# Two local-attention items of a fused attention and two-layer kernel go from the first chunk to the second, and items start every eight steps

## The chip, the cores and the metric

The kernel runs on one core of a Trainium2 chip. The time is device microseconds (us) of one execution, and the number that counts is the median over runs. In the tables and rows PE is the matrix engine (PEld its weight loads), DVE the vector engine, ACT the scalar engine, POOL the GpSimd engine, SP the queue that issues every DMA.

## The reference, cut to what matters

```
q_d, k_d, v_d = means of q, k, v over 4 neighbouring positions     # 576 -> 144 positions
out_d     = softmax(q_d k_d^T / 8) v_d                              # "down" attention
out_local = softmax(where(|i - j| < 4, q k^T / 8, -1e9)) v          # "local" attention
x = repeat(out_d, 4) + out_local            # 4 batches x 8 heads x 576 x 64 -> 2304 x 512
h = x @ w_in;  x = (h - tanh(h)) @ w_out                            # 512 -> 2048 -> 512
out = (sigmoid(x @ w_gate) * (x @ w_val)) @ w_out2                  # 512 -> 1536 -> 512
```

All of it is float32. A product is made as three passes (high x high, high x low, low x high parts).

## The kernel before, in words

The 2304 rows of x are cut into six chunks of 384. For each chunk the first layer runs 16 blocks f: `do_h` makes 12 matmuls of 384 columns (lines 293 to 295, `ab<-x,w`) into one of four PSUM banks called `ab`; ACT takes the tanh (line 718, `t<-ab`), DVE subtracts it (line 306, `t<-ab,t`, which frees the bank), ACT and DVE split the result into high and low part (line 303 `g<-t`, line 306 `g<-t,g`), and two blocks later (`LAG`) `do_y` makes 12 more matmuls (`acc<-g,w`). In this text these are the product matmuls. The second layer follows after the sixth chunk and is not touched.

The attention that makes x runs between the product matmuls. Two heads are a pair, and a batch has four pairs. Its work is a list of 40 **items**: a "d" item (function `down`) does the down attention of one pair, an "l" item (function `local`) does six blocks of 64 rows of local attention, of one pair or of two. An item has a front part, the **scores** on PE (line 403 for d, line 501 for l), and a back part, the **values** on PE (line 464 for d, line 583 for l), with a softmax on DVE and ACT between them. The values need the softmax turned. In the first chunk (`dense`) PE turns it: for an l item `turn` makes two threes of transposes (line 574). In later chunks a DMA does it: DVE sorts the 16-bit halves into a buffer (line 381 `flip<-pl`), SP issues a DMA_TRANSPOSE (line 390), and `join` copies the result back on ACT and DVE (lines 303 and 381, `pt<-flip`, `pdt<-flip`).

Time in the program is counted in **steps** (`tick`): a step follows every six product matmuls, four per block f. `defer(n, ...)` and `chain(n, ...)` put work n steps later; what `chain` brings to a step is written ahead of what `defer` brings. For an l item of a later chunk: scores at step 0, mask and maximum at 2, the exponentials on ACT at 3 (line 561), normalising at 6, the DMA at 8, the join at 12, the values at the first item start from step 14 on. For a d item the join is at 11. PE's order is chosen by a scheduler when the program is built; from the second chunk on, those of ACT, DVE, POOL and SP follow the recorded order.

`work` starts an item when it is due and when the last one is some steps old: `item` returns that distance, seven steps in later chunks, 4 and 6 in the first. `goal` spreads the items over the chunks: before, 8 items run ahead of the first chunk, 10 in it, then 7, 7 and 8 in the second to fourth. When the last item of a chunk's rows is stored, the chunk's x is loaded (`x_load`, line 694); ahead of block 14 the program takes empty steps until that can be done.

`fetch` loads queries and keys of a pair (line 319, `qk`, three buffers) and its values for the down attention (line 324, `vr`). The sums over four neighbours of q and k (`mean_qk`) are one DVE instruction in the first chunk (line 340) and three POOL instructions later (lines 342 to 344); `mean_v` is three more on POOL. There is one buffer `m` for the sums, and `fetch` waits while it is taken. In batch 1, l items cover blocks 0 to 2 of two pairs together, then blocks 3 to 8 of each pair.

Of the kernel before, what the change touches and what calls it, by code (L numbers as in the profile page):

```python
# [29 lines left out]
NQB = S // QB  # L30
# [6 lines left out]
LAST = NC - 1  # L37
# [28 lines left out]
def tile_kernel(ctx: ExitStack, tc: tile.TileContext, qk, vp, v, w1, w2, mask, ident, out):  # L66
# [31 lines left out]
    startup, dense, spare = [True], [True], [0]  # L98
# [16 lines left out]
    now = [0]  # L115
# [3 lines left out]
    def defer(n, fn, *args):  # L119
        events.setdefault(now[0] + n, []).append((fn, args))  # L120
# [10 lines left out]
    def run_later(kind=None, age=0):  # L131
        for x in list(waiting):
            if now[0] >= x[0] + age and kind in (None, x[1]):
                waiting.remove(x)
                x[2]()
# [162 lines left out]
    qks, means, vds, outd = {}, {}, {}, {}  # L298
# [17 lines left out]
    def load_qk(u):  # L316
        if u != (0, NP - 1):
            qks[u] = ap.tile([128, 2, S], F32, tag="qk", bufs=3, name="qk")
        nc.sync.dma_start(out=qks[u], in_=qk[u[0], u[1]])

    def load_v(u):
        vds[u] = ap.tile([72, 2, 128], F32, tag="vd", bufs=2, name="vd")
        vr = ap.tile([72, 2, FAC, 128], F32, tag="vr", name="vr")
        nc.sync.dma_start(out=vr, in_=vp[u[0], u[1]])
        return vr

    def load_pair(u, d):
        load_qk(u)
        vr = load_v(u)
        defer(d, mean_qk, u)  # L330
        defer(d, mean_v, u, vr)

    summed = {}

    def mean_qk(u):
        summed[u] = now[0]
        m = means[u] = ap.tile([128, 2, SD], F32, tag="m", bufs=1, name="m")
        t = qks[u].rearrange("p i (j r) -> p i j r", r=FAC)
        if dense[0]:
            nc.vector.tensor_reduce(out=m, in_=t, op=ALU.add, axis=AX.X)  # L340
        else:
            nc.gpsimd.tensor_tensor(out=m, in0=t[:, :, :, 0], in1=t[:, :, :, 1], op=ALU.add)
            nc.gpsimd.tensor_tensor(out=m, in0=m, in1=t[:, :, :, 2], op=ALU.add)
            nc.gpsimd.tensor_tensor(out=m, in0=m, in1=t[:, :, :, 3], op=ALU.add)
# [141 lines left out]
    def local(us, n):  # L486
        b, p = us[0]
        two = len(us) == 2
        nb_ = LB // len(us)
# [3 lines left out]
        for x in (0, 3, 1, 4, 2, 5):  # L493
# [3 lines left out]
            for h in range(2):  # L497
                r0 = 64 * h
                o0 = 64 - r0 if x >= 3 and four else r0
                bank, at = (sb[x // 3], x % 3) if four else (sb[0], x)  # L500
# [1 line left out]
                    out=bank[o0:o0 + 64, at, :], lhsT=t[r0:r0 + 64, 0, QB * j:QB * j + QB],  # L502
                    rhs=t[r0:r0 + 64, 1, w0:w0 + WIN], start=True, stop=True,
                )
        if n + nb_ == NQB:
            for u in us:
                done_with(u)
        elif not two:
            pass
# [123 lines left out]
    items = []  # L633
    for b in range(B):
        for p in range(0, NP, 2):
            us = ((b, p), (b, p + 1))
# [5 lines left out]
    items[:n_first + 2] = [x for x in items[:n_first + 2] if x[0] == "d" or x[2] == 0] + [  # L642
        x for x in items[:n_first + 2] if x[0] == "l" and x[2]
    ]
    started, fetched, last_fetch = [0], [n_first + 2], [-9]
    live = {(0, p) for p in range(NP - 1)}

    def done_with(u):
        live.discard(u)
# [5 lines left out]
    def fetch():  # L655

        while not startup[0] and fetched[0] < min(len(items), started[0] + 6):
            x = items[fetched[0]]
            if x[0] == "d" and x[1] != (0, 0):
                if len(live) == 3 or len(vds) == 2 or len(means) == 1 or now[0] < last_fetch[0] + 6:  # L660
                    break
                last_fetch[0] = now[0]
                live.add(x[1])
                load_pair(x[1], 4)
            fetched[0] += 1

    def item():

        fetch()
        x = items[started[0]]  # L670
        if x[0] == "d" and (x[1] not in means or now[0] < summed[x[1]] + (0 if startup[0] else 5 if dense[0] else 2)):
            return 0
        started[0] += 1
        run_later()
        if x[0] == "d":
            down(x[1])
            if not dense[0]:
                fetch()
            return 4 if dense[0] else 7
        local(*x[1:])  # L680
        return 6 if dense[0] else 7

    def needed(c):

# [135 lines left out]
    while any(((1, 0), k) not in xt for k in range(KD)):  # L820
        keep_warm(2)
        if started[0] < n_first:
            x = items[started[0]]
# [185 lines left out]
    for c in range(NC):  # L1009
        if c == 0:  # L1010
            in_order(E.SP)
        elif c == 1:
            in_order(E.SP, E.Activation, E.DVE, E.Pool)
            flip_room()
        first = started[0]
        dense[0] = c == 0
        goal = max(needed(min(c + 1, LAST)), first + (len(items) - first) // max(LAST - 1 - c, 1))
        if c == LAST:
            goal = len(items)
        beat[0] = lambda a=(now[0], first, goal, c): work(*a)  # L1020
        for f in range(NE if c == 0 else 0, F1):
            if f == 14 and c < LAST:
                while x_left[c + 1]:
                    tick()
                x_load(c + 1, xd[c + 1])
            do_h(c, f)
            if c == 0 and f == NE:
                todo += [(0, e) for e in range(NE)]
            todo.append((c, f))
            while len(todo) > LAG:  # L1030
                do_y(*todo.pop(0))
# [219 lines left out]
    for j in range(NJ):  # L1251
        for p in range(len(PAIRS)):
            cycle[:] = now[0], p
            for side in range(2):
# [10 lines left out]
                for n, (a, b, at) in enumerate(PRODUCTS):  # L1265
                    for k in range(2):
                        x = xform[p, k, b]
# [47 lines left out]
    for q, (p, e) in enumerate(passes):  # L1315
        ends = None
        for i in range(NJ if q < len(passes) - 1 else NJ - 1):
# [6 lines left out]
            for n, (a, b) in enumerate(order_b):  # L1324
                for m in both:
                    x, w = u_forms[p, m, b], w_sets[e, m]
# [86 lines left out]
```

## Time and profile before

| | |
|---|---|
| median of 3 runs | 911.87 us (911.01 to 913.51) |
| profiled execution | 912.07 us, its span 910.3 us |
| PE busy | 898.2 us (99%) |
| DVE, ACT, POOL busy | 620.7, 463.8, 169.3 us |
| granted PE clock | 0.999 of full speed |
| DMA | 151.13 MB, 166 GB/s on average |

The span is what the engines show from the first to the last instruction; about 1.8 us of the execution lie around it. PE counts as busy while an instruction of it is in the pipeline, so a busy PE can still start its instructions later than it could: how far apart they start is read from the timeline.

### The profile page before, as it was taken

What the parts mean: (1) busy time and instruction counts of PE and PEld (TensorE: products, weight loads), DVE (VectorE), ACT (ScalarE), POOL (GpSimd) and SP (SyncE); (2) the same over time, 40 slices, a digit from 0 to 9 for tenths busy, and PEclk for the clock granted to TensorE, in tenths of its full rate; (3) what the DMA queues carried; (4) which work ended last, traced back from release to release, by engine and by line L of the source; (5) the groups of instructions that cost most, each with busy time, mean ns of one, the idle gap of its engine ahead of it and who ended that gap; (6) DMA issues with size and microseconds to landing.
All of it is one profiled execution on the core that took longest, in us unless ns stands there. A gap on an engine that the chain in (4) does not pass through costs nothing.

```text
span 910.3 us, 16518 instructions
## 1 busy us (share of the span) xinstructions
PE 898.2 (99%) x6260; PEld 865.4 (95%) x6260; DVE 620.7 (68%) x1063; ACT 463.8 (51%) x1128; POOL 169.3 (19%) x186
## 2 busy tenths in 40 slices
PE   7999999999999999999999999999999999999998
PEld 7788989999899999999999999999999999999998
DVE  5799975655554656567865587676858678978581
ACT  4887865444544545434544545353444446655440
POOL 2321110302222020000032352313131323200000
PEclk9999999999999999999999999999999999999999
DMA  8476656353454544468422235343425268896961
GB/s 294 148 239 232 226 158 127 93 123 91 104 117 112 118 98 99 163 235 311 140 67 68 72 137 173 121 154 122 168 107 179 99 206 304 311 313 232 342 201 37
DMA packets 106927, 151.13 MB, mean 166 GB/s; under 512 B 41104, under 2 KB 92896, under 8 KB 102496
## 3 DMA queue, kind: packets, MB, share of 16 engines
q1 hardware_dynamic: 106848, 150.08, 51.7%
q8 instruction: 49, 0.80, 0.4%
q14 instruction: 30, 0.25, 0.1%
HBM read 97.76 MB, written 43.65 MB: 155 GB/s over the span
## 4 chain that ended last, share of the span: by engine, by line
PE 85%; issue 5%; ACT 3%; DVE 3%; DMA 2%; POOL 1%; SPq 1%; POOLq 0%; DVEq 0%; ACTq 0%
PE ab L293 13%; PE acc L293 13%; PE ab L294 13%; PE ab L295 13%; PE acc L295 13%; PE acc L294 12%; PE ab L583 2%; PE ab L501 1%; ACT pl L561 1%; PE ab L403 1%; PE acc L816 1%; PE ab L464 1%; POOL t L1065 1%; DMA u<-t 1%; DMA o<-o 1%
## 5 line engine op out<-in xcount | busy, mean ns | idle before, releaser
L293 PE MATMUL acc<-g,w 128*128 128x384 f32 x384 | 130.7, 342 | 0.0
L293 PE MATMUL ab<-x,w 128*128 128x384 f32 x376 | 129.6, 345 | 0.6 <-DVE t L306 0.6
L295 PE MATMUL acc<-g,w 128*128 128x384 f32 x384 | 129.7, 338 | 0.0
L294 PE MATMUL acc<-g,w 128*128 128x384 f32 x384 | 129.2, 336 | 0.0
L294 PE MATMUL ab<-x,w 128*128 128x384 f32 x376 | 126.5, 336 | 0.0
L295 PE MATMUL ab<-x,w 128*128 128x384 f32 x376 | 126.4, 336 | 0.0
L306 DVE TENSOR_TENSOR t<-ab,t 128x384 f32<-128x384 f32 x94 | 52.0, 553 | 101.6 <-ACT t L718 100.3
L718 ACT ACTIVATE t<-ab 128x384 f32<-128x384 f32 x94 | 45.7, 486 | 120.3 <-PE ab L295 117.1
L295 PE MATMUL ab<-x,f 128*128 128x384 f32 x261 | 87.8, 336 | 0.9 <-DVE f L1127 0.9
L293 PE MATMUL ab<-x,f 128*128 128x384 f32 x261 | 87.8, 337 | 0.0
L293 PE MATMUL acc<-x,f 128*128 128x384 f32 x261 | 87.7, 336 | 0.0
L295 PE MATMUL acc<-x,f 128*128 128x384 f32 x261 | 87.7, 336 | 0.0
L294 PE MATMUL ab<-x,f 128*128 128x384 f32 x261 | 87.6, 336 | 0.0
L294 PE MATMUL acc<-x,f 128*128 128x384 f32 x261 | 87.6, 336 | 0.0
L306 DVE TENSOR_TENSOR g<-t,g 128x384 fp32r<-128x384 f32 x96 | 57.3, 598 | 31.8 <-ACT g L303 30.8
L303 ACT ACTIVATE g<-t 128x384 fp32r<-128x384 f32 x96 | 50.0, 522 | 48.0 <-DVE t L306 48.0
L293 PEld LDWEIGHTS ab<-x,w 128*128 128x128 f32 x376 | 70.6, 188 | 3.8 <-issue 1.0
L293 PEld LDWEIGHTS acc<-g,w 128*128 128x128 f32 x384 | 72.1, 188 | 1.8 <-issue 1.0
L295 PEld LDWEIGHTS acc<-g,w 128*128 128x128 f32 x384 | 72.2, 188 | 0.4 <-issue 0.2
L294 PEld LDWEIGHTS acc<-g,w 128*128 128x128 f32 x384 | 72.2, 188 | 0.3 <-issue 0.2
L294 PEld LDWEIGHTS ab<-x,w 128*128 128x128 f32 x376 | 70.7, 188 | 0.1
L295 PEld LDWEIGHTS ab<-x,w 128*128 128x128 f32 x376 | 70.7, 188 | 0.0
(193 smaller groups left out, 2019.2 us busy)
## 6 DMA issues: line engine op xcount, KB each, us to landing
raw<-in_w SPq DMA_DIRECT2D x34, 1024.0 KB
u<-t SPq DMA_DIRECT2D x51, 192.0 KB
qk<-in_qk SPq DMA_DIRECT2D x16, 576.0 KB
x<-u SPq DMA_DIRECT2D x9, 960.0 KB
o<-o SPq DMA_DIRECT2D x18, 448.0 KB
u<-c SPq DMA_DIRECT2D x39, 192.0 KB
u<-c SPq DMA_DIRECT2D x18, 384.0 KB
o<-f SPq DMA_DIRECT2D x6, 896.0 KB
```

Source lines behind the costliest of these rows:

```text
L293: nc.tensor.matmul(out=o, lhsT=wh, rhs=xh, start=first, stop=False, **kw)
L294: nc.tensor.matmul(out=o, lhsT=wh, rhs=xl, start=False, stop=False, **kw)
L295: nc.tensor.matmul(out=o, lhsT=wl, rhs=xh, start=False, stop=last, **kw)
L303: nc.scalar.activation(out=dst, in_=src, func=ACTF.Copy)
L306: nc.vector.tensor_tensor(out=dst, in0=a, in1=b, op=ALU.subtract)
L403: nc.tensor.matmul(out=sd[t][o0:o0 + 64, at, :], lhsT=qd[r0:r0 + 64, 40 * j:40 * j + 64], rhs=kd[r0:r0 + 64, :], start=True, stop=True,)
L464: nc.tensor.matmul(out=ob[64 * h:64 * h + 64, :], lhsT=vd[:, f, 64 * h:64 * h + 64], rhs=pdt[:, f, h].rearrange("p j k -> p (j k)"), start ...
L501: nc.tensor.matmul(out=bank[o0:o0 + 64, at, :], lhsT=t[r0:r0 + 64, 0, QB * j:QB * j + QB], rhs=t[r0:r0 + 64, 1, w0:w0 + WIN], start=True, ...
L561: nc.scalar.activation(out=pl[:, j, :], in_=pl[:, j, :], func=ACTF.Exp, bias=nb[:, j:j + 1], accum_out=ssum[:, j:j + 1],)
L583: nc.tensor.matmul(out=ob[r0:r0 + 64, QB * x:QB * x + QB], lhsT=vw[0][:, j - n, i, r0:r0 + 64], rhs=pt[:, x, o0:o0 + 64], start=True, stop ...
L718: nc.scalar.activation(out=t, in_=hb[:, :N], func=ACTF.Tanh)
L816: nc.tensor.matmul(out=idle[:, :128], lhsT=id_sb, rhs=id_sb, start=True, stop=True)
```

## The change

The l items of batch 1, pairs 0 and 1, blocks 3 to 8 (`away`), leave their place and stand directly ahead of the same items of pairs 2 and 3, in the second chunk. The q and k of the two pairs are given up after their first l item (`done_with`) and loaded a second time. From the second chunk on `goal` is the whole list and the distance of items is eight steps. A pair is loaded while the one buffer for sums is still taken, and the sum waits for it (`mean_qk_when_free`).

```diff
@@ load_pair @@
-        defer(d, mean_qk, u)
+        defer(d, mean_qk_when_free, u)
         defer(d, mean_v, u, vr)
...
+    def mean_qk_when_free(u):
+        if len(means) == 1:
+            defer(1, mean_qk_when_free, u)
+        else:
+            mean_qk(u)
@@ local @@
-        if n + nb_ == NQB:
+        if n + nb_ == NQB or us == ((1, 0), (1, 1)):
             for u in us:
                 done_with(u)
@@ the list of items @@
+    away = [("l", ((1, p),), 3) for p in range(2)]
+    rest = [x for x in items if x not in away]
+    at = rest.index(("l", ((1, 2),), 3))
+    items[:] = rest[:at] + away + rest[at:]
@@ fetch @@
             x = items[fetched[0]]
+            if x in away:
+                if len(live) == 3 or now[0] < last_fetch[0] + 6:
+                    break
+                last_fetch[0] = now[0]
+                live.add(x[1][0])
+                load_qk(x[1][0])
             if x[0] == "d" and x[1] != (0, 0):
-                if len(live) == 3 or len(vds) == 2 or len(means) == 1 or now[0] < last_fetch[0] + 6:
+                if len(live) == 3 or len(vds) == 2 or dense[0] and len(means) == 1 or now[0] < last_fetch[0] + 6:
                     break
@@ item @@
-            return 4 if dense[0] else 7
+            return 4 if dense[0] else 8
         local(*x[1:])
-        return 6 if dense[0] else 7
+        return 6 if dense[0] else 8
@@ the chunks @@
-        if c == LAST:
+        if c:
             goal = len(items)
```

Counted over the whole program, PE has 12 transposes fewer (line 574), DVE one sum fewer and four copies more, POOL three additions more, SP two loads of q and k (576 KB each) and two DMA transposes more. Lines of the changed kernel after the first edit have numbers 6 to 16 higher.

First place: DVE at the end of the first chunk, from the scores of its last l item on. Before, the mask of that item's scores (line 538) stands behind the sum of the next pair (line 340):

```order
L306 TENSOR_TENSOR g<-t,g 128x384
L420 TENSOR_REDUCE nb<-ab 128x1
L420 TENSOR_REDUCE nb<-ab 128x2
L340 TENSOR_REDUCE m<-qk 128x288
L538 SCALAR_TENSOR_TENSOR pl<-ab,mask_sb 128x210 x2
L357 RECIPROCAL ss<-ss 128x3
L557 TENSOR_REDUCE nb<-pl 128x6
L359 TENSOR_TENSOR pd<-pd,ss 128x432
```

In the changed kernel (line 538 is 544, 557 is 563, 359 is 365):

```order
L306 TENSOR_TENSOR g<-t,g 128x384
L363 RECIPROCAL ss<-ss 128x3
L365 TENSOR_TENSOR pd<-pd,ss 128x432
L544 SCALAR_TENSOR_TENSOR pl<-ab,mask_sb 128x210 x2
L264 TENSOR_TENSOR w<-raw,w 128x1024
L306 TENSOR_TENSOR t<-ab,t 128x384
L563 TENSOR_REDUCE nb<-pl 128x6
L306 TENSOR_TENSOR g<-t,g 128x384
```

The sum is no longer there; it is made by POOL in the second chunk. Between mask and maximum a step of the weights' preparation (line 264) and a product's subtraction now stand.

Second place: ACT in the fourth chunk, around the join of the last d item (`pdt<-flip`) and the exponentials (line 561, 567 in the changed kernel) of the l item after it. Before:

```order
L718 ACTIVATE t<-ab 128x384
L561 ACTIVATE pl,ss<-pl,nb 128x70 x6
L353 ACTIVATE ss<-ss 128x6
L303 ACTIVATE g<-t 128x384
L303 ACTIVATE pdt<-flip 72x2x2x48 x3
L718 ACTIVATE t<-ab 128x384
```

In the changed kernel:

```order
L303 ACTIVATE od<-ab 128x144
L303 ACTIVATE g<-t 128x384
L303 ACTIVATE pdt<-flip 72x2x2x48 x3
L567 ACTIVATE pl,ss<-pl,nb 128x70 x6
L359 ACTIVATE ss<-ss 128x6
L734 ACTIVATE t<-ab 128x384
```

The join has moved from behind the six exponentials to ahead of them.

Third place: SP from the last store of the second chunk's rows (`x_101<-xo`) on. Before:

```order
L310 DMA x_101<-xo 128x2x192
L694 DMA xs<-x_101 128x384 x4
L310 DMA y_86<-y 128x384 x2
L390 DMA_TRANSPOSE flip<-flip 128x12x128
L310 DMA y_86<-y 128x384 x2
```

In the changed kernel (the load of x is line 710):

```order
L310 DMA x_101<-xo 128x2x192
L710 DMA xs<-x_101 128x384 x4
L319 DMA qk<-in_qk 128x1152
L310 DMA y_86<-y 128x384 x2
L396 DMA_TRANSPOSE flip<-flip 128x12x128
L310 DMA y_86<-y 128x384 x2
```

The second load of pair 1's q and k stands behind the load of x; it goes into the buffer that pair 0's moved item has just read.

## Rows read from the trace of the kernel before

**Rows 1.** The page: the span.
```profile
span 910.3 us, 16518 instructions
```
**Rows 2.** Busy by stretch: PE, PEld, DVE, ACT, POOL (instructions), clock, DMA share, GB/s.
```profile
47.00:130.00 83.00, 82.60 (x750) 73.02 (x749) 75.63 (x123) 66.31 (x204) 13.97 (x15) 1.00 0.66 221
134.00:372.00 238.00, 236.83 (x1962) 223.08 (x1962) 135.60 (x295) 117.92 (x411) 37.61 (x42) 1.00 0.46 107
```
**Rows 3.** PE timeline: start, duration, name, count. Values alone, then (293 us) scores alone.
```profile
204.75 0.34 PE L295 MATMUL ab<-x,w 128*128 128x384 f32 x1
205.02 0.92 PE L583 MATMUL ab<-pt,vw 70*64 70x64 f32 x24
205.87 0.44 PE L293 MATMUL ab<-x,w 128*128 128x384 f32 x1
...
293.34 0.34 PE L295 MATMUL ab<-x,w 128*128 128x384 f32 x1
...
294.13 0.45 PE L293 MATMUL ab<-x,w 128*128 128x384 f32 x1
```
**Rows 4.** PE timeline: values and scores as a pair.
```profile
354.48 0.34 PE L295 MATMUL ab<-x,w 128*128 128x384 f32 x1
354.75 0.92 PE L583 MATMUL ab<-pt,vw 70*64 70x64 f32 x24
...
356.13 0.45 PE L293 MATMUL acc<-g,w 128*128 128x384 f32 x1
```
**Rows 5.** PE timeline: the same two, each in two parts, between two products.
```profile
187.50 0.34 PE L294 MATMUL acc<-g,w 128*128 128x384 f32 x1
...
189.55 0.45 PE L295 MATMUL acc<-g,w 128*128 128x384 f32 x1
```
**Rows 6.** PE timeline: one three of transposes in the first chunk.
```profile
90.87 0.34 PE L294 MATMUL ab<-x,w 128*128 128x384 f32 x1
91.04 0.49 PE L574 MATMUL ab<-id_sb,pl 128*70 128x128 f32 x3
91.29 0.42 PE L293 MATMUL acc<-g,w 128*128 128x384 f32 x1
```
**Rows 7.** PE timeline, end of the first chunk.
```profile
125.34 0.34 PE L293 MATMUL acc<-g,w 128*128 128x384 f32 x1
...
126.20 0.34 PE L295 MATMUL acc<-g,w 128*128 128x384 f32 x1
...
129.43 0.45 PE L293 MATMUL ab<-x,w 128*128 128x384 f32 x1
```
**Rows 8.** DVE timeline just ahead of that place.
```profile
121.25 1.34 DVE L340 TENSOR_REDUCE m<-qk 128x288 f32<-128x1152 f32 x1
```
**Rows 9.** PE timeline, second and third chunk: a product, then an item's values.
```profile
242.50 0.34 PE L295 MATMUL acc<-g,w 128*128 128x384 f32 x1
243.43 0.45 PE L293 MATMUL ab<-x,w 128*128 128x384 f32 x1 [0.60 <-DVE t L306]
...
248.57 0.34 PE L295 MATMUL ab<-x,w 128*128 128x384 f32 x1
249.14 1.27 PE L583 MATMUL ab<-pt,vw 70*64 70x64 f32 x24 [0.23 <-ACT pt L303]
```
**Rows 10.** PE timeline: values of two d items.
```profile
170.09 0.72 PE L464 MATMUL ab<-pdt,vd 72*64 72x144 f32 x8
...
345.51 1.30 PE L464 MATMUL ab<-pdt,vd 72*64 72x144 f32 x8
```
**Rows 11.** DVE timeline ahead of 243.43 us.
```profile
239.24 1.14 DVE L306 TENSOR_TENSOR g<-t,g 128x384 fp32r<-128x384 f32 x1 [2.39 <-ACT g L303]
```
**Rows 12.** Groups of DVE instructions, 130 to 375 us: count | busy, mean ns | idle before.
```profile
L306 DVE TENSOR_TENSOR g<-t,g 128x384 fp32r<-128x384 f32 x50 | 29.9, 598 | 26.1 <-ACT g L303 25.7
```
**Rows 13.** SP and POOL timeline: a load of q and k, and its first reader.
```profile
172.48 0.36 SPq L319 DMA_DIRECT2D qk<-in_qk  x1
177.73 0.70 POOL L342 TENSOR_TENSOR m<-qk 128x288 f32<-128x288 f32 x1 [14.26 <-DMA qk<-in_qk]
```

## The prediction

> **What bounds the kernel now.** I read the busy times by stretch first, because the change touches only the stretch from the first chunk to the end of the attention. In the first chunk PE is busy for 82.60 of 83.00 us, in the three chunks behind it for 236.83 of 238.00 us [rows 2]. So PE is the bound, DVE (75.63 of 83.00 us in the first chunk) comes next there, and the idle time of PE in both stretches is 1.57 us. That is not the whole loss, since a busy PE can start late, so I read PE's timeline next. Product matmuls start 0.172 us apart: five intervals from 125.34 to 126.20 us [rows 7]. Wherever attention stands between two of them, its price is the time from the start of the last product matmul ahead to the start of the first one behind, less 0.17 us. Values alone cost 205.87 - 204.75 - 0.17 = 0.95 us, scores alone 294.13 - 293.34 - 0.17 = 0.62 us [rows 3]. As a pair they cost 356.13 - 354.48 - 0.17 = 1.48 us, 0.09 less than apart [rows 4]; with both torn in two they cost 189.55 - 187.50 - 0.17 = 1.88 us, 0.40 more than the pair [rows 5]. A three of transposes costs 91.29 - 90.87 - 0.17 = 0.25 us [rows 6]. What lies above such a price is a stall.
>
> Behind 372 us the program is the same but for a few steps, so the whole effect has to come out of those 325 us.
>
> **The stalls of before.** I went through all 61 places with attention between products; four stand out.
> - End of the first chunk: 129.43 - 126.20 - 0.17 = 3.06 us for the values of a d item (0.72 as a row [rows 10]), two threes of transposes (0.50) and values (0.95), together 2.17. Stall 0.9 us [rows 7]. Ahead of it DVE makes a sum of 1.34 us while the mask of the last item waits behind it [rows 8].
> - At 242.50 us PE starts its next product 0.93 us later, 0.76 too late, because DVE had not freed the bank; ahead of it a DVE subtraction took 1.14 us [rows 9, 11].
> - At 248.57 us the values come 0.57 us behind the product instead of 0.27 (204.75 to 205.02), and then take 1.27 us instead of 0.92: stall 0.65 us [rows 3, 9].
> - At 345.51 us the values of a d item take 1.30 us, at 170.09 us they took 0.72: stall 0.58 us [rows 10].
>
> Together 2.9 us. This and the prices above are all that can be won.
>
> **The change part by part.**
>
> *PE's own work.* Two l items lose their PE transposes: four threes, -1.0 us. All else that PE computes stays, but stands elsewhere. I gave each place in both orders the price of its rows. From the second chunk on, before, scores or values stood alone at eleven places and were torn at three; with eight steps between items, exactly two blocks, values and scores fall together every time, in the middle of a product's 12 matmuls. The sum there is 33.6 us before. The two items that arrive add 2 x (0.95 + 0.62) = 3.1, which makes 36.7; after, it is 35.0, so pairing gives -1.7 us. In the first chunk the sum is 23.0 before, 18.9 without the two items and their transposes, and 20.8 after, because its scheduler now tears more pieces: +1.9 us. The three together: -0.8 us. The bounds are +0.9 (pairing gives nothing) and -2.7 (the torn pieces of the first chunk cost what whole ones do); I take -0.8, since every place has a price of its own.
>
> *The end of the first chunk.* Two l items fewer for DVE, and the sum of 1.34 us goes to POOL, so the last item's mask no longer waits behind it. The stall of 0.9 is shorter than that sum. In its place a weight subtraction stands between mask and maximum, so I take -0.7 us, between -0.9 and 0.
>
> *Eight steps instead of seven.* A step is six product matmuls, 6 x 0.172 = 1.03 us. Values follow their scores by two items, 16 steps instead of 14, so the chain between them has 2.06 us more. The stalls at 248.57 and 345.51 us, 0.65 and 0.58, are waits for the end of that chain. In addition the join of a d item now stands ahead of the next item's exponentials on ACT and not behind them, as the second place of the order shows. Both should go: -1.23 us. The wait at 242.50 us is DVE being late by 0.76; with one step more per item DVE has 1.03 us more for the same work, but POOL's sums can meet DVE again (below). I take -0.5, between -0.76 and 0.
>
> *What is added and hidden.* Two loads of q and k. The second is the tight one: it starts when the first moved item's scores are done and is read by the next item's scores, 48 product matmuls or 8.3 us later. A load reached its reader 177.73 - 172.48 = 5.25 us after its issue [rows 13]. Hidden, with 3.0 us to spare; without that cover PE would stand for what is missing, at most 5.25 us, and SP, with the stores of y queued behind the load, would pass the delay on to the buffers of y. The two additional DMA transposes and four DVE copies meet a DVE that is busy for 135.60 of 238.00 us in that stretch, the three additional POOL additions a POOL busy for 37.61 [rows 2]: nothing, unless they meet a DVE operation on which PE waits.
>
> *The end of the fourth chunk.* The list now ends later: the load of the fifth chunk's x has to wait four empty steps for its last store. The values of the last item but one stand 28 product matmuls (4.8 us) behind the last item's scores, and ahead of their join on ACT lie that item's six exponentials. I put +0.2 us here, between 0 and 3 (rivals).
>
> Sum: -0.8 - 0.7 - 1.23 - 0.5 + 0.2 = -3.0 us. The profiled execution took 912.07 us, of which 910.3 are its span [rows 1]; it stands 0.2 above the median of 911.87. The forecast by the profile is a span of 907.3, an execution of 909.0, and as a median 911.87 - 3.0 = **908.9 us**.
>
> **DVE and POOL.** At 239.24 us a DVE subtraction took 1.14 us while POOL was adding [rows 11]; the mean of its 50 like is 0.598 us [rows 12]. The Trainium skill, page "SBUF — State Buffer", section "Who interferes with whom", says that a DVE instruction with two inputs from SBUF and a GpSimd instruction that reads SBUF exclude each other for the whole instruction, and that a reduction on trn2 never contends. The long subtraction agrees. The rule speaks against this change, which turns one DVE reduction into three POOL additions and keeps seven other sums on POOL: by it one more stall like the one of now may come, 0.76 + 0.65 us, and the sum would be -1.6; by the rows, where seven sums together leave PE idle for 1.2 us at most, it is nothing. The last rival is this mechanism at its full size, priced from rows.
>
> **The rivals.**
> - *The POOL stalls stay.* The sums meet DVE as they do now, so the waits at 242.50 and 248.57 us keep their 0.76 and 0.65. For it: nothing in the change keeps POOL and DVE apart. Against: one step more per item. The sum becomes -3.0 + 0.5 + 0.65 = -1.85: 910.0 us.
> - *The short end takes it back.* The last item but one has only 70 product matmuls and a pair between its scores and values, 70 x 0.172 + 1.48 = 13.5 us. At 248.57 us an item with 84 matmuls, 84 x 0.172 + 1.48 = 15.9 us, was 0.65 too late, so by that measure this one is 2.4 + 0.65 = 3.0 us late. Against it: in the empty steps no tanh or split of a product stands between the parts of the chain. Then -3.0 - 0.2 + 3.0 = -0.2: 911.7 us.
> - *Slower: every sum on POOL costs PE what one costs now.* All items now lie in the same place of a block. If the sums meet DVE in the place that delays the bank, each costs 0.76 + 0.65 = 1.4 us. With n of the eight the time is 911.87 - 3.0 - 0.26 (what the sum still holds of the wait at 242.50 us) + 1.4 n: slower by over 0.3% from n = 5 on, and 919.8 us with all eight. Against it: 42 POOL instructions, seven sums of six, stand in a stretch in which PE is idle for 1.2 us in all [rows 2], so six of seven cost next to nothing.
>
> **How the numbers follow.** The measurement tells a change of about 0.3%, 2.7 us, from none. The forecast holds 0.50, with a range of its own from 907.5 to 910.0, and so is faster than 909.1 in about three cases of four. The POOL stalls have 0.24, the short end 0.14, the slower rival 0.10; 0.02 are for a late load. Faster: 0.38 from the forecast and 0.05 of the first rival, 0.43. Slower: 0.10, and 0.03 for the short end or the load with more than I gave them, 0.13. The same: 0.44. The range goes from 907.2 (all stalls gone, and pieces of the first chunk cheaper than priced) to 912.4 (the short end and some of POOL); what is outside is the slower rival and the tails.
>
> **What would show it.** PE: no transposes of two of the ten l items of the first chunk; from the second chunk on all attention in pairs of 1.3 to 1.6 us, 48 product matmuls apart, with no row of values longer than 0.92 (l) or 0.72 (d). At the end of the first chunk the time from the d item's values to the next product is as long as its pieces. The moved items' scores start without a wait. It would be wrong if product rows wait for `t` on DVE next to POOL rows, if the values near the end of the fourth chunk carry a wait for `pt`, or if the first chunk's PE work grew by more than priced.

## The result, and the profile after

The changed kernel takes 919.58 us, median of four runs (917.93 to 920.99), against 912.27 us (911.01 to 913.51) for the kernel before beside it: ratio 1.0079, 95% interval 1.0054 to 1.0105. It is slower by 7.3 us where 3 us of gain were forecast. The profiled execution took 918.36 us, 1.2 less than the median; its span is 916.3 us, where [rows 1] has 910.3.

First, busy time by stretch, the two stretches of [rows 2] and one of the second layer, with the same columns, and then this third stretch in the kernel before:

```profile
47.00:130.00 83.00, 82.55 (x654) 71.28 (x653) 72.16 (x112) 61.18 (x175) 11.24 (x13) 1.00 0.64 215
134.00:372.00 238.00, 237.76 (x2045) 226.13 (x2046) 140.93 (x306) 121.99 (x436) 42.92 (x48) 1.00 0.51 119
...
525.00:785.00 260.00, 253.28 (x1449) 252.06 (x1448) 193.45 (x300) 118.86 (x191) 82.57 (x91) 0.99 0.46 163
```

```profile
525.00:785.00 260.00, 260.00 (x1499) 259.13 (x1498) 195.49 (x304) 122.50 (x195) 83.60 (x91) 1.00 0.48 167
```

In the two stretches that the change was meant for PE is as busy as before or busier: 237.76 of 238.00 us, where 236.83 stood. The loss is in the third stretch, from 525 us on, which the prediction did not look at. There PE was busy for all of the 260 us in the kernel before; now it is idle for 6.72 us of them.

Second, the last product of the first layer, on PE's timeline, in the kernel before and then in the changed kernel:

```profile
510.01 0.34 PE L295 MATMUL acc<-g,w 128*128 128x384 f32 x1
```

```profile
507.04 0.34 PE L295 MATMUL acc<-g,w 128*128 128x384 f32 x1
```

It starts 2.97 us earlier. So up to here the forecast of 3.0 us came true in this execution. From here to the end of the span it was 910.3 - 510.01 = 400.3 us; now it is 916.3 - 507.04 = 409.3 us. Those 9.0 us, less the 3.0, are the 6.0 by which the span grew. I call the second number the **rest** and give both for every run.

Third, PE's waits in the changed kernel behind the first layer. There are two, of 3.03 and 3.69 us, and both are new. On PE's timeline the brackets give the wait and what ended it:

```profile
527.83 0.34 PE L295 MATMUL ab<-x,f 128*128 128x384 f32 x1
531.20 0.45 PE L293 MATMUL ab<-x,f 128*128 128x384 f32 x1 [3.03 <-DVE two L1061]
...
541.19 0.34 PE L293 MATMUL ab<-x,f 128*128 128x384 f32 x1
545.23 0.45 PE L294 MATMUL ab<-x,f 128*128 128x384 f32 x1 [3.69 <-DVE x L1009]
...
546.64 0.52 PE L295 MATMUL ab<-x,f 128*128 128x384 f32 x1
546.96 0.52 PE L293 MATMUL ab<-x,f 128*128 128x384 f32 x1
...
549.84 0.34 PE L293 MATMUL ab<-x,f 128*128 128x384 f32 x1
```

These are the first products of the second layer (`x` is the first layer's result in the forms that the second layer multiplies, `f` its weights). The first wait costs 531.20 - 527.83 - 0.17 = 3.20 us, the second 545.23 - 541.19 - 0.17 = 3.87 us. Behind the second, ten products from 546.64 to 549.84 us start 0.32 us apart and not 0.172: another 1.48 us. The window of that stretch shows why, in its granted clock (the 0.66):

```profile
545.00:550.00 5.00, 4.77 (x18) 4.78 (x19) 3.04 (x5) 0.49 (x1) 3.54 (x3) 0.66 0.58 219
```

3.20 + 3.87 + 1.48 = 8.55 of the 9.0 us of this execution.

Fourth, what PE waited for. DVE's timeline in the changed kernel ahead of the first wait's end, and ahead of the second's:

```profile
526.78 1.37 DVE L1009 TENSOR_TENSOR x<-t,x 128x384 fp32r<-128x384 f32 x1
528.07 1.34 DVE L1009 TENSOR_TENSOR x<-xs,x 128x384 fp32r<-128x384 f32 x1
529.34 1.34 DVE L1002 TENSOR_TENSOR x<-t,x 128x384 fp32r<-128x384 f32 x1
530.60 0.54 DVE L1061 TENSOR_TENSOR two<-ab,two 128x384 f32<-128x384 f32 x1
...
540.79 1.56 DVE L1108 TENSOR_TENSOR c<-c 128x768 f32<-128x768 f32 x1
...
542.74 1.09 DVE L1009 TENSOR_TENSOR x<-t,x 128x384 fp32r<-128x384 f32 x1
543.76 0.95 DVE L1108 TENSOR_TENSOR c<-c 128x768 f32<-128x768 f32 x1
544.63 0.55 DVE L1009 TENSOR_TENSOR x<-xs,x 128x384 fp32r<-128x384 f32 x1
```

and in the kernel before (line 993 there is 1009 here, 986 is 1002, 1092 is 1108, 1045 is 1061) ahead of the second place:

```profile
538.95 0.71 DVE L993 TENSOR_TENSOR x<-t,x 128x384 fp32r<-128x384 f32 x1
...
540.05 0.54 DVE L993 TENSOR_TENSOR x<-xs,x 128x384 fp32r<-128x384 f32 x1
540.52 0.95 DVE L1092 TENSOR_TENSOR c<-c 128x768 f32<-128x768 f32 x1
```

`x<-t,x` and `x<-xs,x` make the forms of x; `c<-c` is the second layer's gating product; `two<-ab,two` takes a finished sum out of a PSUM bank and so frees it. DVE takes its work in program order. At the second place that order differs. Before, `x<-t,x` and `x<-xs,x` stand ahead of both gating products. Now the first stands behind one of them and the second behind both, and PE's wait ends with that second one (544.63 + 0.55). From the first form there to the end of this one DVE takes 8.0 us (537.19 to 545.18), where it took 5.2 (535.38 to 540.59).

At the first place the order differs too, but DVE takes no longer. PE's wait ends with `two` (530.60 + 0.54). The first form there and `two`, in the kernel before, and the first form in the changed kernel:

```profile
520.68 1.77 DVE L993 TENSOR_TENSOR x<-xs,x 128x384 fp32r<-128x384 f32 x2 [2.46 <-ACT x L303]
...
530.42 0.54 DVE L1045 TENSOR_TENSOR two<-ab,two 128x384 f32<-128x384 f32 x1
```

```profile
520.94 2.42 DVE L1009 TENSOR_TENSOR x<-xs,x 128x384 fp32r<-128x384 f32 x2
```

From one to the other it is 10.3 us before and 10.2 now. But counted from the last product of the first layer it starts at 13.9 us and not at 10.7, and this 3.2 us is the wait. At both places DVE's rows in the changed kernel leave no gap from the first form to the end of PE's wait, so what starts late there ends late.

The cause of both lies in the program. The forms are made by the preparation of the second layer (`second_weights` and `forms_of_x`, which proceed step by step beside the first layer, at a rate `RATE`). `work` lets it begin when the last attention x has been stored. With the items' distance at eight steps the list ends later: counted in the program, the preparation now begins at step 328 and not 324, while the fifth chunk begins at 322 and not 321. Against PE that is three steps, of 1.03 us each, less of a lead (at the last loads of y, at step 474 and not 471, it is two, since the products stand a step later too). That was the theory to test.

### The profile page after: what moved, and what is told of

It is laid out like the page before. It is cut to its first block, busy times and chain, and to the rows that moved or that the text cites. A ratio compares the mean times of both kernels' runs of the same rounds, so it can differ in the third digit from the quotient of the medians.

```text
span 916.3 us, 16519 instructions
## 1 busy us (share of the span) xinstructions
PE 897.9 (98%) x6248; PEld 864.3 (94%) x6248; DVE 629.7 (69%) x1066; ACT 462.7 (50%) x1126; POOL 174.4 (19%) x189
## 4 chain that ended last, share of the span: by engine, by line
PE 84%; DVE 5%; issue 4%; DMA 3%; ACT 2%; POOL 1%; SPq 1%; POOLq 0%; DVEq 0%; ACTq 0%
PE ab L293 13%; PE acc L293 13%; PE ab L295 13%; PE acc L294 13%; PE ab L294 13%; PE acc L295 13%; PE ab L589 2%; PE ab L507 1%; PE ab L470 1%; PE ab L409 1%; PE acc L832 1%; DMA o<-o 1%; DMA u<-t 1%; POOL t L1081 1%; DVE x L1009 1%
```

## The experiments

In each, the time from the span's start to the last first-layer product and the rest tell the two halves of the program apart.

**The delay alone, in the kernel before, and the lead given back, in the changed kernel.** The first edit holds the preparation back by three steps, the second runs it a little faster:

```diff
-        if "f" not in wpools and not any(x_left[1:]):
+        if "f" not in wpools and not any(x_left[1:]) and now[0] >= 327:
```

> The kernel before, with one condition: the preparation of the second layer starts at step 327 and not at 324, three steps later against PE, as in the changed kernel. Nothing in the attention changes. Theory A: the first layer is as before, and waits of 6 to 9 us appear around 530 to 550 us: 918 to 921 us. Rival B: the first layer does not end sooner, so nothing waits: 912 us.

```diff
-RATE = 0.55
+RATE = 0.57
```

> The changed kernel, with one number changed: RATE, which sets how much of the second layer's preparation a step of the fifth and sixth chunk takes, 0.57 instead of 0.55. The order then has the last load of y for the forms of x three steps sooner and ahead of the first stores of u, as before the change. Theory A (the preparation starts three steps later against PE and arrives late at two places): the two waits at 527.8 and 541.2 us, 3.2 and 3.9 us, and the stretch at half clock behind them go, the first layer keeps its gain of 3.4: about 909 us, between 908 and 910.5. Rival B (the entry of the second layer waits for something with a time of its own, so whoever ends the first layer sooner waits there): the waits stay, about 919 us.

The delay made the kernel before slower: 922.30 us, ratio 1.0116 (1.0100 to 1.0132), with the last product at 509.37 us and a rest of 413.0 us. Its PE waits show the same two places (line waited at, releaser: us in total, times, longest):

```profile
PE ab L293 <- DVE two L1045: 3.0, 1, 3.0
PE ab L294 <- DVE x L993: 2.8, 1, 2.8
```

Here the clock fell behind both of them, to 0.66 on average from 530 to 540 us and to 0.85 from 550 to 560 us. The first of these windows:

```profile
530.00:540.00 10.00, 6.97 (x25) 6.65 (x25) 5.89 (x9) 2.54 (x4) 5.81 (x6) 0.66 0.56 198
```

The changed kernel with the rate 0.57 takes 909.45 us, ratio 0.9971 (0.9958 to 0.9983) to the kernel before. The last product starts at 506.64 us, and the rest is 401.9 us. From 525 to 785 us PE waits for 1.0 us in all, 0.6 behind the entry (for ACT's `one`) and 0.4 for `two`.

So the delay of the preparation makes such a loss in a kernel whose attention is unchanged, and giving the changed kernel its lead back takes 7.4 us off its rest (409.3 to 401.9; with the rate 0.56 below, 9.5 us).

**Is the 0.57 worth something by itself?** The kernel before with `RATE = 0.57`.

> The kernel before with the rate 0.57 and nothing else. It tells whether the 2.6 us that the changed kernel with 0.57 is below the kernel before are the change's gain in the first layer or the rate's. Theory A (in the kernel before the preparation is early enough already; the gain is that the first layer ends 3 us earlier): no gain from the rate, 911.5 to 913.5 us, the last product of the first layer near 510 us. Rival (an earlier preparation is worth something by itself): 909 to 910.5 us.

912.20 us, ratio 1.0000 (0.9987 to 1.0012); last product 509.54 us, rest 399.4 us. The rival falls: the 2.6 us that the changed kernel with 0.57 gains come from its first layer.

**The parts of the change.** First the move of the items and the second load alone, then only the eight steps and the goal, then the whole change without the eight steps:

```diff
 # the move alone, against the changed kernel
-        defer(d, mean_qk_when_free, u)
+        defer(d, mean_qk, u)
-                if len(live) == 3 or len(vds) == 2 or dense[0] and len(means) == 1 or now[0] < last_fetch[0] + 6:
+                if len(live) == 3 or len(vds) == 2 or len(means) == 1 or now[0] < last_fetch[0] + 6:
-            return 4 if dense[0] else 8
+            return 4 if dense[0] else 7
-        return 6 if dense[0] else 8
+        return 6 if dense[0] else 7
-        if c:
+        if c == LAST:
             goal = len(items)
```

> The changed kernel's move of the two items and their second loads alone: seven steps between items, goals and the wait of loads for sums as before. The preparation starts at step 321 with the fifth chunk at 318, three steps behind it as before the change. Theory A: no wait at the entry of the second layer; the first layer wins the end of the first chunk and the transposes but not the pairing: about 910.5 us, 909 to 912. Rival B: what the first layer wins is lost again at the entry, 912 or more.

```diff
 # eight steps and the goal alone, against the kernel before
-            return 4 if dense[0] else 7
+            return 4 if dense[0] else 8
-        return 6 if dense[0] else 7
+        return 6 if dense[0] else 8
-        if c == LAST:
+        if c:
             goal = len(items)
```

> The kernel before with eight steps between items and the whole list as goal from the second chunk on; no item moved, loads wait for sums as before. The 22 items end earlier than before, the preparation starts nine steps sooner against PE. Theory A: no wait at the entry, the stalls of the third to fourth chunk (2.0 us) and some tearing go: about 909.5 us, 908.5 to 911. Rival B: 912 or more. If eight steps themselves cost time, more than 912 with waits ahead of 372 us.

```diff
 # all but the eight steps, against the changed kernel
-            return 4 if dense[0] else 8
+            return 4 if dense[0] else 7
-        return 6 if dense[0] else 8
+        return 6 if dense[0] else 7
```

> The changed kernel, but items seven steps apart again in place of eight; the move, the goals and the loads that don't wait for sums stay. The items end earlier, so the preparation of the second layer begins some twenty steps earlier. Theory A (the loss is the late preparation): no PE wait at 528 and 541 us. What the eight steps are worth in the first layer stands against that: if the stalls of seven steps (some 2 to 3 us over chunks two to four, as the run of the move alone had) come back, the last product of the first layer begins near 509 to 510 us and the time is 911 to 913 us; if the loads that don't wait for sums suffice without the eight steps, that product begins at 507 us and the time is near 909.5 us.

The move alone: 914.67 us, ratio 1.0030 (1.0015 to 1.0045); last product 512.22 us, rest 400.6 us. Eight steps alone: 913.33 us, ratio 1.0008 (0.9992 to 1.0025); 510.53 and 399.4 us. All but the eight steps: 917.58 us, ratio 1.0055 (1.0037 to 1.0073); 513.33 and 399.4 us. None of the three waits at the entry of the second layer, as expected. But the two with seven steps lose in the first layer, eight steps alone are level with the kernel before, and the numbers I had put on them, 909.5 to 913 us, were missed by all; for eight steps alone it came as the last sentence of the expectation has it, more than 912 us with waits ahead of 372 us.

The rows say where. With the move alone PE waits at several places for a softmax that is not finished (0.2 to 0.3 us each) and for DVE; the longest:

```profile
234.90 0.45 PE L293 MATMUL ab<-x,w 128*128 128x384 f32 x1 [0.73 <-DVE t L306]
```

With eight steps alone, where a pair's load still waits for the buffer of sums, PE waits twice for POOL's sums, 3.5 us together; the first:

```profile
215.24 0.71 PE L403 MATMUL ab<-m 64*64 64x144 f32 x12 [1.94 <-POOL m L344]
```

Without the eight steps the longest wait is for the turned softmax, and a stretch of half clock (starts 0.32 us apart from 169.75 us on) follows it:

```profile
167.56 1.27 PE L589 MATMUL ab<-pt,vw 70*64 70x64 f32 x24 [1.30 <-ACT pt L303]
```

The profiled execution of this one, 914.96 us, was the lowest of its ten, so its rows show the least of its loss; where the others spend up to 5 us more stays open. What follows: the parts don't add up. The move loses with seven steps (last product 2.2 and 3.3 us later than in the profiled execution of before), eight steps without loads that go ahead of their sums gain nothing, and the three together gain.

**How much delay, and what it acts through.** The kernel before with one and with two steps of delay, that is, with `now[0] >= 325` and `now[0] >= 326` in the condition above:

> The kernel before, with the preparation of the second layer held back by one step instead of three. The last four loads of y then stand behind two stores of u in SP's queue, not behind six. If the wait grows with the steps of delay, from none at zero to about 3 us at each of two places at three: about 1 us at each place, 913.5 to 915 us. If there is slack of a step or two and then an edge (the loads' place among the stores): no wait, 912 us as the kernel before.

> The kernel before, with the preparation held back by two steps. One step gave one wait of 0.9 us at the second place (542 us) and none at the first, three steps 3.2 and 3.0 us. If the wait follows the delay step by step (a step is six products of 173 ns, 1.0 us): 1.5 to 2.5 us at the second place and 0.5 to 2 us at the first, 915 to 918 us. If the order of loads and stores in SP's queue set it (at two steps it is that of three steps): 3 us at both places, 920 to 922 us.

One step: 914.04 us, ratio 1.0013 (1.0000 to 1.0027), rest 401.9 us. Two: 920.58 us, ratio 1.0095 (1.0074 to 1.0115), rest 409.0 us. PE's wait at the entry with one step and then with two:

```profile
PE ab L294 <- DVE x L993: 0.7, 1, 0.7
```

```profile
PE ab L294 <- DVE x L993: 5.2, 1, 5.2
```

Neither expectation for two steps was right. The loss does not follow the delay evenly: 1.6 us of rest for the first step, 7.1 for the second, 4.0 for the third (from 400.3 to 401.9, 409.0 and 413.0 us; the runs with no wait at the entry have 399.4 to 400.6). The run with three steps was profiled in the slowest of its four executions, 924.21 us; by the medians, each against the kernel before beside it, the losses are 0.9, 8.7 and 10.3 us, so the third step adds 1.6 us and not 4.0.

The changed kernel's 409.3 us is that of two steps in its sum, but not in its pattern, since with two steps the first place has no long wait. The program has the reason. The loads of y for the first place stand at step 457 in the kernel before, at 458, 459 and 460 with one to three steps of delay, and at 461 in the changed kernel, whose fifth chunk begins one step later: against PE it is three steps late there, as with the delay of three, and those two have the first wait. At the last loads of y (473 with two and with three steps, 474 in the changed kernel) all three are two steps late.

What the second step costs at the second place is in part seen on DVE's timelines. With one step:

```profile
540.69 0.95 DVE L1092 TENSOR_TENSOR c<-c 128x768 f32<-128x768 f32 x1
...
542.03 1.11 DVE L993 TENSOR_TENSOR x<-xs,x 128x384 fp32r<-128x384 f32 x1
```

With two:

```profile
541.37 1.52 DVE L1092 TENSOR_TENSOR c<-c 128x768 f32<-128x768 f32 x1
...
543.29 1.10 DVE L993 TENSOR_TENSOR x<-t,x 128x384 fp32r<-128x384 f32 x1
544.30 0.95 DVE L1092 TENSOR_TENSOR c<-c 128x768 f32<-128x768 f32 x1
545.17 0.55 DVE L993 TENSOR_TENSOR x<-xs,x 128x384 fp32r<-128x384 f32 x1
```

With one step of delay `x<-xs,x` stands behind one gating product, with two behind both. The queue of SP changes at the same point, though: with two steps, as in the changed kernel, the last four loads of y (from which the forms are made) stand behind six stores of u, and in this run they also come late. POOL waits for them (in the changed kernel for 0.46 us only), and DVE then stands idle ahead of its first form:

```profile
536.78 1.02 POOL L974 TENSOR_TENSOR t<-xs 128x384 f32<-128x384 f32 x1 [4.81 <-DMA xs<-y]
```

```profile
537.72 1.85 DVE L993 TENSOR_TENSOR x<-xs,x 128x384 fp32r<-128x384 f32 x2 [1.45 <-ACT x L303]
```

So here both have a part in the 5.2 us, and this pair alone doesn't tell the two apart.

**SP's order or DVE's.** Two edits of the changed kernel, in both of which the preparation stays late. The first puts the loads of y ahead of the stores again, by issuing the first stores later:

```diff
+        first = (j, p) == (0, 0)
-        if not last:
+        if not last and not first:
             store(to[:, 0, :], b11)
...
-            if last:
+            if last or first:
                 store(to[:, 0, :], b11)
...
-        defer(4 if last else 1, stores)
+        defer(4 if last else 3 if first else 1, stores)
```

> The changed kernel, but the first two stores of u (and the four behind them) are issued behind the sums of the second half, so that all eight loads of y for the last forms of x stand ahead of them in SP's queue again, as in the kernel before. The preparation still ends three steps late. Theory A1 (the wait at 541 us is the loads of y that stand behind the stores of u; the wait at 528 us is VectorE's copy `two` that stands behind four subtractions): the PE wait near 541 us (3.9 us) and the stretch of half clock behind it (about 1.6 us) go, the wait near 528 us (3.2 us) stays: 914 to 916 us. Theory A2 (both waits come from the late preparation alone, whatever the order of loads and stores): both waits stay, 918.5 to 920 us.

The second puts the gating products (`done`) three steps later as long as the forms are not finished:

```diff
-        yield lambda: (add(c[0][:, 1, :], bank[1], three), defer(1, done, 0))
-        yield lambda: (add(c[1][:, 0, :], bank[2], three), defer(1, done, 1))
+        yield lambda: (add(c[0][:, 1, :], bank[1], three), defer(1 if 2 in formed else 4, done, 0))
+        yield lambda: (add(c[1][:, 0, :], bank[2], three), defer(1 if 2 in formed else 4, done, 1))
```

> The changed kernel (preparation still three steps late), but while the forms of x are unfinished the gating products of the first pairs (two c<-c of 0.95 us and more each on VectorE, and their four sums on POOL) stand three steps later in the program, so that at both places the subtractions that make the forms of x stand ahead of them on VectorE. Theory (what is late is the place of the subtractions in VectorE's order, behind copies and products of the second layer that it takes first): the wait at 541 us falls from 3.9 us to 0 to 1.5 us, that at 528 us from 3.2 to 0.5 to 1.5 us, since the subtractions then also run without POOL beside them (0.55 in place of 1.34 us); the half clock behind them goes; 911 to 914 us. Rival (the chain from the loads of y over POOL's sums sets when the forms can be made): both waits stay, 918 to 920 us.

The first gave 918.06 us, ratio 1.0063 (1.0041 to 1.0085), rest 408.0 us. All eight loads of y stand ahead of the stores of u, and both waits are there:

```profile
510.80 21.95 SPq L983 DMA_DIRECT2D xs<-y  x8
532.79 11.37 SPq L310 DMA_DIRECT2D u<-c  x7
```

```profile
PE ab L293 <- DVE two L1061: 3.0, 1, 3.0
PE ab L294 <- DVE x L1009: 2.8, 1, 2.8
```

So the theory that the second wait of the changed kernel comes from SP's order falls: it is 0.9 us shorter, but it stays.

The second gave 911.98 us, ratio 0.9990 (0.9977 to 1.0004); last product 508.80 us, rest 401.4 us. Of the two long waits one of 1.3 us is left, and the clock does not fall (1.00 from 540 to 550 us):

```profile
PE ab L294 <- DVE x L1009: 1.3, 1, 1.3
```

DVE's timeline at the first place has the forms ahead now:

```profile
527.55 0.55 DVE L1009 TENSOR_TENSOR x<-xs,x 128x384 fp32r<-128x384 f32 x1
528.02 0.54 DVE L1002 TENSOR_TENSOR x<-t,x 128x384 fp32r<-128x384 f32 x1
528.49 0.94 DVE L1108 TENSOR_TENSOR c<-c 128x768 f32<-128x768 f32 x1
529.36 0.54 DVE L1061 TENSOR_TENSOR two<-ab,two 128x384 f32<-128x384 f32 x1
```

This edit also issues the stores of u later, but the run before shows that this alone does nothing here. With the same lateness and another order on DVE, 7.9 of the 9.0 us are gone (a rest of 401.4 and not 409.3 us). At the first place DVE starts as late as in the changed kernel (14.0 us behind the last product), but has `two` done after 7.1 us and not 10.2. POOL's differences of u move back together with the gating products, and 1.8 of these 3.1 us come from the three subtractions, two of which now run without POOL beside them (see below). So the run shows that the place of the gating work sets the loss, but not how much of it is DVE's order alone.

**How early is early enough.** The changed kernel with `RATE = 0.56` and with `RATE = 0.6`:

> The changed kernel with the rate 0.56, which brings the last loads of y one step behind their place in the kernel before instead of three. If the wait follows the delay: none at 528 us, up to 1 us at 541 us, and with a first layer that ends near 507 us a time of 909 to 911 us; if any delay behind the kernel before brings both waits: 915 us or more.

> The changed kernel with the rate of the preparation at 0.60 in place of 0.55, which ends it some five steps earlier than the kernel before did, where 0.57 ended it about one step earlier. If all that the changed kernel lacked is an early enough preparation, both waits stay gone and the time is that of 0.57: 908.5 to 910.5 us. If a denser preparation takes VectorE's and POOL's time from the last items of the first layer, the last product of the first layer begins later than 506.6 us, and the time lies by as much above 909.5 us.

909.18 us, ratio 0.9966 (0.9951 to 0.9980), rest 399.8 us; and 911.04 us, ratio 0.9980 (0.9963 to 0.9996), rest 400.4 us. No long wait at the entry in either. At 0.56 the last loads of y come one step later than in the kernel before, but so do the products, so by that count nothing is late, and nothing waits. The three rates' intervals overlap; 0.56 and 0.57 stand below the kernel before by about 0.3% and below the changed kernel by 1.1%, 0.60 below the kernel before by 0.2%. At 0.60 the fifth and sixth chunk take 1.3 us longer than in the changed kernel (table below), as the second half of its expectation has it.

## Why the prediction was wrong, by its own steps

**The step that failed** is the sentence "Behind 372 us the program is the same but for a few steps, so the whole effect has to come out of those 325 us." The few steps were the effect: 9.0 us of rest, against 3.0 us won. I had read that the list ends later and costed it only where it ends (+0.2 us, for the load of the fifth chunk's x). I did not ask what else begins at the list's end: the preparation of the second layer does. No term, bound or rival of the prediction contained it, and the range ended at 912.4 us. That the slower rival's price for all eight sums, 919.8 us, is near the result is no support for it: its mechanism did not happen (below).

**The first layer.** The sum, -3.0 us, measured -2.97 in the profiled pair and -2.6 us as a median, with the rate 0.57, which avoids the loss behind it. One execution is a rough witness for it, however: the last product starts between 508.98 and 511.26 us in the five profiled executions that have the first layer of before, 509.8 on average, and between 506.64 and 509.12 us in the six that have the changed one, 507.9 on average. That makes 1.9 us, so that the pair came so near to -3.0 is in part luck. Where the difference arises is read from the start of DVE's first copy of each chunk's y (line 755, in the changed kernel 771), which comes when the chunk's products end. For the first chunk, before and after:

```profile
144.82 0.55 DVE L755 COPY y<-acc 128x384 f32<-128x384 f32 x1
```

```profile
141.78 0.55 DVE L771 COPY y<-acc 128x384 f32<-128x384 f32 x1
```

| us | end of the first chunk | second to fourth | fifth and sixth |
|---|---|---|---|
| kernel before, profiled | 144.82 | 235.58 | 128.94 |
| mean of the five | 145.12 (144.58 to 146.32) | 235.03 | 129.02 |
| changed kernel, profiled | 141.78 | 235.65 | 128.94 |
| mean of the six | 142.49 (141.39 to 143.88) | 235.63 | 129.26 |
| changed kernel, rate 0.60 | 141.64 | 235.66 | 130.26 |
| the move alone | 142.49 | 240.12 | 128.94 |
| eight steps alone | 144.27 | 236.83 | 128.76 |
| all but the eight steps | 140.98 | 243.07 | 128.61 |

What varies most is the first chunk; with the rate 0.56, to name the worst, PE was idle there for 2.73 us, mostly waiting for DVE at line 443 (1.7 us). Behind it the second to fourth chunk repeat within 0.9 us in the five and within 0.2 in the six.

- *Pairing.* As forecast: from the second chunk on, scores and values stand together, 48 product matmuls apart, with one torn at 372 us.
- *The end of the first chunk.* The stall of [rows 7] is gone. In the changed kernel the last values there cost 125.36 - 124.25 - 0.17 = 0.94 us, the price of values alone [rows 3]:

```profile
124.25 0.33 PE L295 MATMUL acc<-g,w 128*128 128x384 f32 x1
...
125.36 0.45 PE L293 MATMUL ab<-x,w 128*128 128x384 f32 x1
```

- *Eight steps.* The waits of [rows 9, 10] are gone; from 134 to 372 us PE waits in one line only:

```profile
PE ab L589 <- ACT pt L303: 0.2, 1, 0.2
```

- *The short end.* That 0.2 us is it, at 364.11 us; +0.2 was the term, and the rival's 3.0 us did not come.
- *POOL and DVE, the slower rival.* No product of that stretch waits for `t` on DVE. POOL does lengthen DVE's work, but at a place that I had not looked at, the entry of the second layer, and with the second layer's own differences, not with the sums of the attention.
- *The terms.* By place the forecast held: it was -2.9 us in the first chunk (from 23.0 to 20.8, and -0.7) and -0.1 behind it (+1.4 from 33.6 to 35.0, -1.73, +0.2). Measured were -3.0 and +0.1 in the pair, -2.6 and +0.6 as means. Split by edit it does not hold. The pairing of -1.7 needs the eight steps too, so the forecast has the move with seven steps at +0.2 (-1.0 + 1.9 - 0.7) and the eight steps behind it at -3.2. The runs show the move with seven steps behind the kernel before, by 2.4 or 3.5 us at the last product against the mean of 509.8, and the eight steps worth 5.4 us behind that (513.3 to 507.9). The first chunk gains as forecast in both; the second to fourth take 4 to 8 us longer than in either kernel. I had priced eight steps against the stalls of the kernel before, but the two added items make new stalls with seven. The waits and the clock in the rows above are a part of those; the rest stays open.

**What lengthened the waits.** While POOL made its four differences of u, from 526.00 to 531.53 us in the changed kernel, the subtractions of the forms took 1.34 to 1.37 us, and the three ahead of `two` 4.05 us together. In the run with the gating products later POOL was idle from 527.21 to 529.58 us, and the two subtractions there took 0.54 to 0.55; the one ahead of them, at 526.45 us with POOL at work, took 1.18. `two`, which has only one input in SBUF, took 0.54 with POOL beside it. The Trainium skill, page "SBUF — State Buffer", section "Who interferes with whom", says that a DVE instruction with two SBUF inputs contends with a GpSimd instruction that reads SBUF, and these rows agree. The kernel before has such subtractions there as well (1.37 us at 529.13), so this lengthens the waits but does not make the difference between the two kernels.

```profile
526.00 5.53 POOL L1081 TENSOR_TENSOR c<-c 128x384 f32<-128x384 f32 x4
```

## What to carry to other kernels

Where work is released by an event (the last store, a buffer that comes free), a change that moves the event moves all that it releases: follow it to its first reader, even where no instruction of that later part was edited, and compare the order on each engine there too. On an engine that keeps the program's order a delay of two steps can cost far more than its length of 2.06 us (8.7 us here, where one step cost 0.9 and three 10.3, by the medians), since the late instruction falls behind others and its input behind other transfers. And price an edit against the schedule in which it will stand: eight steps were worth far more with the moved items than without.

## What was not expected of the hardware

- Behind waits of PE of 3 to 5 us in the second layer the granted clock fell, from the 2.4 GHz level to the 1.2 GHz level as the starts 0.32 and 0.172 us apart show: 0.66 as the mean of 545 to 550 us in the changed kernel. The length of the wait alone did not decide it. In the changed kernel the clock held behind the first wait of 3.0 us and fell behind the second of 3.7; with the delay of three steps it fell behind both, with the stores later it fell behind the first of 3.0 and held behind the second of 2.8. It held at 1.00 behind the single waits of 0.7 and 1.3 us in the second layer and behind one of 1.9 us with eight steps alone (215.24 us), and fell behind one of 1.3 us in the run without the eight steps (167.56 us). It cost 1.5 us in the changed kernel, a sixth of its loss.
- The first chunk's stalls differ by up to 2.5 us between profiled executions whose first layer is the same (PE idle from 47 to 130 us for 0.21 us at the rate 0.57, 2.73 at 0.56), so a single pair of profiles does not settle an effect of 2 us there.
